# Other booked times for GpSimd, later sums of the key features, and another order of the last head's first products

## The chip, the cores and the metric

The kernel runs on one core of a Trainium2 chip. The metric is device time in microseconds (us) of one execution. A core has five engines that work at the same time and wait for each other through semaphores: TensorE (PE, matrix products), VectorE (DVE), ScalarE (ACT), GpSimd (POOL) and SyncE (SP, which issues DMAs; GpSimd issues some too). Each engine takes its own instructions in the order in which they were written.

## What is computed

The input is x (1 x 2048 x 1024), two sets of weights, and a gate vector. Block A is attention with a linear feature map, block B is softmax attention with 32 heads of 32 columns each, and a gate mixes both row by row:

```python
def _A_ref(x, wqkv, wo):          # H = 32, Dh = 32
    q, k, v = qkv[0], qkv[1], qkv[2]
    phi = lambda t: jnp.where(t > 0, t + 1, jnp.exp(t)) + 1e-6
    pq, pk = phi(q), phi(k)
    kv = jnp.einsum("bhsd,bhse->bhde", pk, v)
    z = jnp.einsum("bhsd->bhd", pk)
    num = jnp.einsum("bhqd,bhde->bhqe", pq, kv)
    den = jnp.einsum("bhqd,bhd->bhq", pq, z)[..., None] + 1e-6
    o = num / den
...
def _B_ref(x, wqkv, wo):
    scores = jnp.einsum("bhqd,bhkd->bhqk", q, k) * (Dh ** -0.5)
    p = _softmax(scores, axis=-1)
    o = jnp.einsum("bhqk,bhkd->bhqd", p, v)
...
g = _sigmoid((x * gate_w).sum(-1, keepdims=True))
return g * _A_ref(x, A_wqkv, A_wo) + (1 - g) * _B_ref(x, B_wqkv, B_wo)
```

## The kernel before

Up to about 620 us the kernel makes block B's q, k and v. From there on four kinds of work are woven into one another on TensorE, and the last stretch makes the output:

- `maxima`: score products (line 1440) whose maxima VectorE takes (1445), so that the exponentials stay small.
- `heads_`: for each of the 32 heads the score products (1581), the exponentials on ScalarE (1584) into nine buffers, the `pr` slots (big_5128 to big_5136), and the products of those with v (1731, in `av`), 16 blocks t of 128 keys in two calls, `av(0, 8)` and `av(8, 16)`, but in the last head in calls of four blocks.
- `linear`: block A's products. A weight is split into a rounded part and a rest, so every product takes three matmuls (lines 154, 157 and 159), and they come in chunks: key and value chunks kv0 to kv3, then the queries, then the output.
- the stores and the output stage.

The softmax's denominators are made with GpSimd's help. For each head it adds the exponentials of all blocks into one buffer `lacc` (big_5137 and big_5138 by turns): `first` (line 1662) adds blocks 0 and 1, `more` (1666) the rest, 128 x 1536 at a time, and the last four blocks in parts of 128 x 512; VectorE adds the remaining 512 columns. In heads 0 to 13 and 19 to 29 two DMAs that GpSimd issues (1620 and 1621, the "fold") then add one half of the partitions to the other, and TensorE sums over the partitions with small products against ones (1504, in `finish`). In the other heads `finish` reads the unfolded sums (1496). A head's `finish` is put into a list `ends` and is run at the start of the next head's `av(0, ...)`, so TensorE comes to it after it has done a good part of the next head's scores.

GpSimd also does three other things here: the rests of the weights at a change of chunk (`split_w`, 1054, behind a cast by ScalarE in 1052, eight of each at a change, each gated by TensorE's last use of the weight that is replaced; four changes: kv1 to kv2, kv2 to kv3, kv3 to the queries, and between the queries' two chunks), the sums of the key features (1331, or a copy in 1329 for a chunk's first block), and small sums for the gate (759).

Nothing of this order is fixed by hand. A planner in Python walks through the work and keeps a clock for each engine: `use(engine, cost, *after)` books a duration on the engine's clock T and gives back the time at which the result is there. GpSimd's additions are kept in a list `sums_left`, and `add_now` writes the next one when GpSimd's clock is no further than TensorE's; so the booked durations of GpSimd decide where its additions stand between the other work, and where the scores, products and finishes come on TensorE. `fold_now` writes a fold when its additions are booked as done, and books 6 us more until it has landed. The order is the only thing that the clocks leave in the program: what an engine really waits for is decided on the chip.

## Time and profile before

| | us |
|---|---|
| median of 3 runs | 2820.77 |
| lowest and highest | 2820.20 and 2821.47 |
| the profiled execution, its time | 2822.18 |
| the profiled execution, its span | 2820.4 |
| busy: TensorE | 2796.0 |
| busy: VectorE | 2268.8 |
| busy: GpSimd | 2102.9 |
| busy: ScalarE | 1662.6 |

The span is the time from the first to the last instruction in the trace. The profiled execution is 1.8 us longer than its span, and 1.4 us above the median. In the profile a row of the timeline has the start in us, the time that the row takes, the engine, the line, the operation and its tiles, how many instructions it holds (x3), and in brackets how long the engine was idle before it and what ended that. The table by windows gives for each stretch the busy time of each engine and the granted TensorE clock (PEclk, 1.00 is full speed). The waits are listed by who waited for whom, with the sum, the number and the longest of them.

### The profile page before, as it was taken

The numbers are of one execution on the slowest core, as the hardware profiler recorded it, in microseconds if no ns is written. First come the engines' busy times: TensorE is split into PE (matmuls) and PEld (weight loads), VectorE is DVE, ScalarE is ACT, GpSimd is POOL, SyncE is SP. The second block draws the span as 40 slices with busy tenths as digits, with TensorE's granted clock in tenths as the row PEclk, the third lists the DMA queues.
The fourth block names the chain that finished last, engine by engine and source line by source line (L and its number), as shares of the span: only waits on it lengthen the run. The fifth ranks groups of instructions, "written<-read, shape, count | busy, mean of one in ns | idle before, by whom it ended". The sixth has DMA issues, their size and how long they took to land.

```text
span 2820.4 us, 46781 instructions
## 1 busy us (share of the span) xinstructions
PE 2796.0 (99%) x15784; PEld 2010.3 (71%) x15784; DVE 2268.8 (80%) x3713; ACT 1662.6 (59%) x3170; POOL 2102.9 (75%) x1145
## 2 busy tenths in 40 slices
PE   9999999999999999999999999999999999999999
PEld 8888888886666666676676777667666666666587
DVE  6697759688877888788888778777888888887678
ACT  4343433347666666676776667667767667676522
POOL 0152026459999999999999789989999999999100
PEclk9999999999999999999999999999999999999999
DMA  8588749673433334333344456656544454334674
GB/s 269 166 275 281 225 143 283 218 234 90 123 84 84 92 99 111 93 98 89 88 117 129 152 158 193 183 170 195 136 108 131 107 162 107 92 106 126 233 232 155
DMA packets 391291, 432.77 MB, mean 153 GB/s; under 512 B 105550, under 2 KB 237902, under 8 KB 389260
## 3 DMA queue, kind: packets, MB, share of 16 engines
q1 hardware_dynamic: 367116, 389.27, 45.9%
q0 software_dynamic: 21632, 36.32, 6.1%
q10 hardware_dynamic: 2304, 4.20, 0.4%
q8 instruction: 126, 2.06, 0.3%
q14 instruction: 113, 0.93, 0.1%
HBM read 287.31 MB, written 127.93 MB: 147 GB/s over the span
## 4 chain that ended last, share of the span: by engine, by line
PE 90%; DVE 4%; POOL 3%; DMA 2%; ACT 1%; issue 1%; SPq 0%; DVEq 0%; POOLq 0%; ACTq 0%
PE bank L1731 15%; PE bank L1581 15%; PE bank L1440 15%; PE bank L154 12%; PE bank L157 12%; PE bank L159 12%; PE bank L644 5%; POOL big L1666 3%; DVE mx L1445 2%; DMA big<-ra 1%; PE bank L1504 1%; PE bank L1234 1%; DVE big L1903 1%; DMA big<-big 1%; ACT big L1584 1%
## 5 line engine op out<-in xcount | busy, mean ns | idle before, releaser
L1666 POOL TENSOR_TENSOR big<-big,big 128x512 f32<-128x512 f32 (+2 forms) x694 | 1643.7, 2372 | 61.0 <-ACT big L1584 15.0
L1445 DVE TENSOR_REDUCE mx<-bank 128x1 f32<-128x512 f32 x2048 | 1283.1, 682 | 280.6 <-PE bank L1440 278.3
L1584 ACT ACTIVATE big<-bank 128x512 f32<-128x512 f32 x2048 | 1151.7, 604 | 334.2 <-PE bank L1581 276.1
L1440 PE MATMUL bank<-big,big 128*128 128x512 f32 x1888 | 738.0, 393 | 2.9 <-ACT big L1584 2.2
L1581 PE MATMUL bank<-big,big 128*128 128x512 f32 x1888 | 736.4, 395 | 3.6 <-ACT big L1584 2.9
L154 PE MATMUL bank<-big,big 128*128 128x512 f32 x1408 | 552.8, 393 | 2.6 <-ACT big L304 1.4
L157 PE MATMUL bank<-big,big 128*128 128x512 f32 x1408 | 549.7, 390 | 0.0
L159 PE MATMUL bank<-big,big 128*128 128x512 f32 x1404 | 548.2, 390 | 1.1 <-DVE big L299 1.1
L1731 PE MATMUL bank<-big,mid 128*32 128x512 f32 x4096 | 457.6, 596 | 0.0
L1581 PEld LDWEIGHTS bank<-big,big 128*128 128x128 f32 x1888 | 353.3, 188 | 128.6 <-issue 43.6
L1440 PEld LDWEIGHTS bank<-big,big 128*128 128x128 f32 x1888 | 354.4, 188 | 84.1 <-ACT big L1584 7.7
L1731 PEld LDWEIGHTS bank<-big,mid 128*32 128x32 f32 x4096 | 133.8, 110 | 281.9 <-issue 279.9
L154 PEld LDWEIGHTS bank<-big,big 128*128 128x128 f32 x1408 | 264.8, 188 | 66.8 <-ACT big L1584 5.2
L159 PEld LDWEIGHTS bank<-big,big 128*128 128x128 f32 x1404 | 263.7, 188 | 57.3 <-DVE big L299 2.4
L157 PEld LDWEIGHTS bank<-big,big 128*128 128x128 f32 x1408 | 264.9, 188 | 55.2 <-DVE big L299 0.2
L1682 DVE TENSOR_TENSOR bank<-bank,big 128x512 f32<-128x512 f32 x364 | 252.2, 693 | 13.6 <-ACT big L1584 6.4
L304 ACT CAST big<-mid 128x512 fp32r<-128x512 f32 (+1 forms) x169 | 100.5, 619 | 138.1 <-DVE mid L1850 72.4
L299 DVE TENSOR_TENSOR big<-mid,big 128x512 fp32r<-128x512 f32 (+1 forms) x138 | 96.1, 712 | 78.6 <-ACT big L304 78.1
L644 PE MATMUL bank<-big,big 128*128 128x512 f32 x672 | 152.6, 389 | 0.0
L1662 POOL TENSOR_TENSOR big<-big,big 128x1536 f32<-128x1536 f32 (+1 forms) x31 | 132.9, 4288 | 24.0 <-ACT big L1584 24.0
L644 PEld LDWEIGHTS bank<-big,big 128*128 128x128 f32 x672 | 126.1, 188 | 26.2
L1739 ACT COPY mid<-bank 128x512 f32<-128x512 f32 x32 | 18.8, 588 | 207.9 <-PE bank L1731 180.5
(197 smaller groups left out, 2424.5 us busy)
## 6 DMA issues: line engine op xcount, KB each, us to landing
big<-xs SPq DMA_DIRECT2D x202, 256.0 KB
big<-qk SPq DMA_DIRECT2D x705, 64.0 KB
qk<-mid SPq DMA_DIRECT2D x128, 256.0 KB
xh<-xs SPq DMA_DIRECT2D x102, 256.0 KB
big<-oA SPq DMA_DIRECT2D x86, 256.0 KB
xs<-big SPq DMA_DIRECT2D x64, 256.0 KB
oA<-mid SPq DMA_DIRECT2D x64, 256.0 KB
big<-big POOLq DMA_DIRECT2D x50, 256.0 KB, 5.0
```

Source lines behind the costliest of these rows:

```text
L154: yield nc.tensor.matmul(ps, sh, mh_, start=(kt == 0), stop=False)
L157: yield nc.tensor.matmul(ps, sh, ml_, start=False, stop=(late and last))
L159: yield nc.tensor.matmul(ps, sl, mh_, start=False, stop=last)
L644: nc.tensor.matmul(bank[at + i], x_, w_, start=(kt == u == 0 and not onto), stop=(kt == KH - 1 and u == 2), skip_group_check=onto)
L1440: nc.tensor.matmul(bank[b], q[:, t % TPC * P:(t % TPC + 1) * P], k[:, j * C:(j + 1) * C], start=True, stop=True)
L1445: nc.vector.tensor_reduce(m[:, t, j:j + 1], bank[b], AX.X, ALU.max)
L1581: nc.tensor.matmul(bank[b], k[:, t * P:(t + 1) * P], q_cols(h, j), start=True, stop=True)
L1584: nc.scalar.activation(pr_t[i][:, j * C:(j + 1) * C], bank[b], AF.Exp, scale=SCALE)
L1662: nc.gpsimd.tensor_add(lacc[:, :qp], pr(0)[:, :qp], pr(1)[:, :qp])
L1666: nc.gpsimd.tensor_add(lacc[:, sl], lacc[:, sl], pr(t)[:, sl])
L1682: nc.vector.tensor_add(lacc[:, qp:] if t == NT - 1 else l_b[:, :n], l_b[:, :n], src)
L1731: nc.tensor.matmul(av_b[j * DH:(j + 1) * DH, :], v[:, t, :], pr(t)[:, j * C:(j + 1) * C], start=(t == 0), stop=(t == NT - 1))
```

## The change

Three edits.

The first is to durations that the planner books for GpSimd: a weight's rest 1.23 to 1.35; a key feature's sum 0.69 to 0.78; the two fold DMAs 2.0 to 2.45; `first` 0.15 to 0.96 plus 0.0022 for each column (for 1536 columns 3.53 to 4.34); `more` 0.15 to 0.21 plus the same.

The second takes the key features' sums out of the place where VectorE's feature is written, puts them into a list `z_todo`, and writes them in the main loop once TensorE's clock has passed the feature's booked end by 1.5.

The third concerns the last head only. Its first products with v, `av(0, 4)`, no longer wait for the finish of head 30 and no longer run it; that finish is run at the start of `av(4, 8)`.

```diff
-        w_ready[k] = use("dve", 0.6, end) if eng is nc.vector else use("pool", 1.23, end)
+        w_ready[k] = use("dve", 0.6, end) if eng is nc.vector else use("pool", 1.35, end)
...
     z_end = [0.0, 0.0]
+    z_todo = deque()
+
+    def features_now(upto=None):
+        while z_todo and (z_todo[0][0] <= upto if upto is not None else z_todo[0][1] <= T["pe"]):
+            z_todo.popleft()[2]()
...
             e, r = mid[3 + n % 3], mid[6]
+            features_now(n - 3)
...
-                def more(end, c=c, t=t, e=e, ps=ps):
+                def more(end, n=n, c=c, t=t, e=e, ps=ps):
                     pk = e[:, :HC]
                     nc.vector.scalar_tensor_tensor(pk, pk, 1.0, ps[:, :HC], op0=ALU.min, op1=ALU.add)
-                    z_end[c % 2] = use("pool", 0.69, end)
-                    if t == 0:
-                        nc.gpsimd.tensor_copy(zsum[c % 2], pk)
-                    else:
-                        nc.gpsimd.tensor_add(zsum[c % 2], zsum[c % 2], pk)
+                    z_end[c % 2] = None
+
+                    def features():
+                        z_end[c % 2] = use("pool", 0.78, end)
+                        if t == 0:
+                            nc.gpsimd.tensor_copy(zsum[c % 2], pk)
+                        else:
+                            nc.gpsimd.tensor_add(zsum[c % 2], zsum[c % 2], pk)
+
+                    z_todo.append((n, end + 1.5, features))
...
-            mark.end = use("pool", 2.0) + 6.0
+            mark.end = use("pool", 2.45) + 6.0
...
-            return use("pool", 0.15 + qp * 0.0022, at)
+            return use("pool", 0.96 + qp * 0.0022, at)
...
-            return use("pool", 0.15 + (sl.stop - sl.start) * 0.0022, at)
+            return use("pool", 0.21 + (sl.stop - sl.start) * 0.0022, at)
...
         def av(t0, t1):
             blocks_ = range(t0, t1)
+            early = last and t0 == 0
             yield lambda: both(max(pr_end[idx(blocks_[-1])], free[4] if t0 == 0 else 0.0),
-                               *(start() for start, _ in ends))
+                               *(start() for start, _ in ends if not early))
             use("pe", AV_SWITCH, pr_end[idx(blocks_[-1])])
-            while ends:
+            while ends and not early:
                 ends.pop()[1]()
...
         gate_step()
+        features_now()
         fold_now()
```

No engine has an instruction more or less; only the order differs. Lines after the edits are moved: in the changed kernel the finish's products are in lines 1508 and 1516 (before 1496 and 1504), the products with v in 1744 (1731), the fold in 1632 and 1633 (1620 and 1621), `first` in 1674 (1662), `more` in 1678 (1666), the score products in 1452 and 1593 (1440 and 1581), the features' sums in 1341 (1331).

Three places show how the order moves.

GpSimd, second chunk change, of before; head 7's additions go into big_5138, head 8's into big_5137; big_221, big_222, big_1258 and big_3332 hold the weights' parts, two columns each:

```order
L1666 TENSOR_TENSOR big_5138<-big_5138,big_5128 128x512
L1666 TENSOR_TENSOR big_5138<-big_5138,big_5129 128x512
L1620 DMA big_5138<-big_5138 64x4x256
L1621 DMA big_5138<-big_5138 64x4x256
L1662 TENSOR_TENSOR big_5137<-big_5130,big_5131 128x1536
L1054 TENSOR_TENSOR big_221<-big_5140,big_221 128x512
L1331 TENSOR_TENSOR mid_230<-mid_230,mid_227 128x256
L1054 TENSOR_TENSOR big_221<-big_5140,big_221 128x512
L1054 TENSOR_TENSOR big_222<-big_5140,big_222 128x512
```

The same place of the changed kernel, from the seventh of the eight rests (two for each of the four tiles) to the fold:

```order
L1054 TENSOR_TENSOR big_3332<-big_5140,big_3332 128x512
L1678 TENSOR_TENSOR big_5138<-big_5138,big_5135 128x512
L1678 TENSOR_TENSOR big_5138<-big_5138,big_5136 128x512
L1678 TENSOR_TENSOR big_5138<-big_5138,big_5128 128x512
L1678 TENSOR_TENSOR big_5138<-big_5138,big_5129 128x512
L1678 TENSOR_TENSOR big_5138<-big_5138,big_5135 128x512
L1054 TENSOR_TENSOR big_3332<-big_5140,big_3332 128x512
L1678 TENSOR_TENSOR big_5138<-big_5138,big_5136 128x512
L1678 TENSOR_TENSOR big_5138<-big_5138,big_5128 128x512
L1341 TENSOR_TENSOR mid_230<-mid_230,mid_228 128x256
L1678 TENSOR_TENSOR big_5138<-big_5138,big_5129 128x512
L1632 DMA big_5138<-big_5138 64x4x256
```

Before, all of head 7's additions, its fold and head 8's `first` come ahead of the first of the eight rests; in the changed kernel seven rests come ahead of the last eight additions, the eighth stands among them, and the fold stands behind them all.

GpSimd, first chunk change, of before, from head 1's last part of `more` (into big_5138):

```order
L1666 TENSOR_TENSOR big_5138<-big_5138,big_5132 128x512
L1054 TENSOR_TENSOR big_221<-mid_225,big_221 128x512
L1331 TENSOR_TENSOR mid_230<-mid_230,mid_229 128x256
L1620 DMA big_5138<-big_5138 64x4x256
L1621 DMA big_5138<-big_5138 64x4x256
L1054 TENSOR_TENSOR big_221<-big_5140,big_221 128x512
L1054 TENSOR_TENSOR big_222<-big_5140,big_222 128x512 x2
```

The same place of the changed kernel:

```order
L1054 TENSOR_TENSOR big_222<-big_5140,big_222 128x512 x2
L1054 TENSOR_TENSOR big_1258<-big_5140,big_1258 128x512
L1054 TENSOR_TENSOR big_1258<-mid_224,big_1258 128x512
L1054 TENSOR_TENSOR big_3332<-mid_225,big_3332 128x512
L1054 TENSOR_TENSOR big_3332<-big_5140,big_3332 128x512
L1678 TENSOR_TENSOR big_5138<-big_5138,big_5132 128x512
L1632 DMA big_5138<-big_5138 64x4x256
L1633 DMA big_5138<-big_5138 64x4x256
```

The fold moved from behind the first of the rests to behind the last.

TensorE, last head, of before; the finish of head 30 reads big_5137, the last head's products with v go into bank_242:

```order
L159 MATMUL bank_240<-big_1258,big_210 128x512
L1581 MATMUL bank_241<-big_208,big_209 128x512
L154 MATMUL bank_240<-big_1258,big_210 128x512
L157 MATMUL bank_240<-big_1258,big_210 128x512
L1496 MATMUL bank_243<-big_5137,ones 32x512 x4
L1731 MATMUL bank_242<-big_5129,mid_236 32x512 x4
L1731 MATMUL bank_242<-big_5130,mid_236 32x512 x4
L1731 MATMUL bank_242<-big_5131,mid_236 32x512 x4
L1731 MATMUL bank_242<-big_5132,mid_236 32x512 x4
L1581 MATMUL bank_245<-big_208,big_209 128x512
```

The same place of the changed kernel:

```order
L154 MATMUL bank_243<-big_3332,big_210 128x512
L1744 MATMUL bank_242<-big_5129,mid_236 32x512 x4
L1744 MATMUL bank_242<-big_5130,mid_236 32x512 x4
L1744 MATMUL bank_242<-big_5131,mid_236 32x512 x4
L1744 MATMUL bank_242<-big_5132,mid_236 32x512 x4
L1593 MATMUL bank_241<-big_208,big_209 128x512
```

The finish is gone from ahead of the products. It now stands behind 30 more matmuls, ahead of the next four blocks:

```order
L1593 MATMUL bank_243<-big_208,big_209 128x512
L157 MATMUL bank_244<-big_222,big_210 128x512
L159 MATMUL bank_244<-big_222,big_210 128x512
L1508 MATMUL bank_239<-big_5137,ones 32x512 x4
L1744 MATMUL bank_242<-big_5133,mid_236 32x512 x4
```

Two more facts of the changed order are used below. On TensorE, at the first chunk change, the last product with the weight that the eighth rest replaces stands 12 matmuls ahead of head 1's finish. At the second change, the last product with the weight that the seventh rest replaces stands 44 matmuls ahead of head 7's finish, and the last one with the eighth's five matmuls later. On ScalarE, there, the first exponential of head 8 into big_5135 stands between the casts of the seventh and the eighth weight; the score product that needs the bank which it empties comes eight matmuls behind the seventh's last product.

## The prediction

> **What bounds the kernel now.** I read the page's busy times first, then TensorE's waits, then the table by windows at the places of the waits, and there the timelines.
>
> ```profile
> PE 2796.0 (99%) x15784; PEld 2010.3 (71%) x15784; DVE 2268.8 (80%) x3713; ACT 1662.6 (59%) x3170; POOL 2102.9 (75%) x1145
> ```
>
> TensorE works 2796.0 of the span's 2820.4 us, and the change takes no matmul away. So all that an order can win is 24.4 us of idle time and what the clock loses behind it; it can lose any amount. Who TensorE waited for (us, times, longest):
>
> ```profile
> PE bank L1496 <- POOL big L1666: 5.4, 1, 5.4
> PE bank L1581 <- ACT big L1584: 2.9, 1, 2.9
> PE bank L1440 <- ACT big L1584: 2.2, 2, 1.4
> PE bank L1504 <- DMA big<-big: 1.8, 2, 1.1
> ```
>
> The windows show where, and that the clock falls behind each:
>
> ```profile
> core 0: us, PE busy (x) PEld busy (x) DVE busy (x) ACT busy (x) POOL busy (x), PEclk, DMA share, GB/s
> 764.00:784.00 20.00, 18.10 (x132) 9.02 (x131) 11.41 (x20) 9.42 (x20) 19.84 (x13) 0.91 0.45 103
> 796.00:804.00 8.00, 7.06 (x26) 4.14 (x25) 6.96 (x13) 3.84 (x8) 7.76 (x4) 1.00 0.14 40
> 1136.00:1156.00 20.00, 15.71 (x128) 9.32 (x130) 11.90 (x22) 10.27 (x22) 19.92 (x14) 0.91 0.44 116
> 2608.00:2624.00 16.00, 10.56 (x62) 5.02 (x61) 16.00 (x17) 6.96 (x15) 7.42 (x2) 0.89 0.91 318
> 2674.00:2690.00 16.00, 13.69 (x59) 10.37 (x58) 8.00 (x13) 4.34 (x8) 0.00 (x0) 1.00 1.07 356
> 650.00:1510.00 860.00, 850.76 (x5322) 572.95 (x5315) 708.40 (x1230) 581.89 (x1139) 833.69 (x413) 1.00 0.37 98
> ```
>
> Three places hold most of the loss: the first chunk change (idle 20 - 18.10 = 1.9 us), the second (4.3) and the last head (5.4). From 650 to 1510 us GpSimd works 833.69 of 860 us, so there it is nearly as full as TensorE, and where its work stands in its queue decides who waits.
>
> What a fallen clock costs is seen in the same 64 products with v, behind the first wait and undisturbed:
>
> ```profile
> 774.85 8.75 PE L1731 MATMUL bank<-big,mid 128*32 128x512 f32 x64
> ...
> 2595.47 0.39 PE L1581 MATMUL bank<-big,big 128*128 128x512 f32 x1
> 2595.70 0.39 PE L159 MATMUL bank<-big,xh 128*128 128x512 f32 x1
> 2596.02 7.07 PE L1731 MATMUL bank<-big,mid 128*32 128x512 f32 x64
> ```
>
> 8.75 - 7.07 = 1.7 us for one fall. I take 1.7 for each wait of about 2 us or more (1.9 was enough at 774 us); the 1.2 and 1.1 us from 2674 to 2690 us cost no clock (1.00):
>
> ```profile
> 2677.71 0.50 PE L154 MATMUL bank<-big,big 128*128 128x512 f32 x1 [1.19 <-ACT big L304]
> 2688.01 0.50 PE L159 MATMUL bank<-big,big 128*128 128x512 f32 x1 [1.12 <-DVE big L299]
> ```
>
> **The booked times.** What GpSimd's work takes, by the starts of neighbours:
>
> ```profile
> 953.15 1.01 POOL L1620 DMA_DIRECT2D big<-big x1 [0.30 <-POOL big L1666]
> 954.43 4.28 POOL L1662 TENSOR_TENSOR big<-big,big 128x1536 f32<-128x1536 f32 x1
> 957.89 1.51 POOL L1331 TENSOR_TENSOR mid<-mid,mid 128x256 f32<-128x256 f32 x1
> 944.83 8.02 POOL L1666 TENSOR_TENSOR big<-big,big 128x512 f32<-128x512 f32 x6
> 763.42 1.30 POOL L1054 TENSOR_TENSOR big<-mid,big 128x512 fp32r<-128x512 f32 x1
> 764.68 0.74 POOL L1331 TENSOR_TENSOR mid<-mid,mid 128x256 f32<-128x256 f32 x1
> ```
>
> A part of 512 takes 8.02 / 6 = 1.34 us; the new booking, 0.21 + 512 x 0.0022 = 1.34, meets it (the old said 1.28). A rest takes 764.68 - 763.42 = 1.26, booked 1.35. But the fold and `first` take 957.89 - 953.15 + 0.30 = 5.0 us together, and are booked at 2.45 + 4.34 = 6.8 (before 2.0 + 3.53 = 5.5). The 4.28 shown for `first` holds time that the fold's DMAs took from it; the next instruction starts 3.46 us after it. Over a head (12 parts and 10 long additions, each now booked 0.06 dearer) the old bookings ran short by about 22 x 0.06 - 0.5 = 0.8 us, and the new ones are 1.8 us too long. So the planner thought GpSimd ahead of where it was, and now thinks it behind: after five heads by about 9 us. It no longer writes GpSimd's additions where GpSimd could take them, but later, and puts other work in front.
>
> The Trainium skill, page "Perfetto Trace Analysis", section "GPSIMD Engine Instruction", says that a GpSimd span in a profile isn't to be trusted and that the spacing of starts is. By the span of 4.28 the booked 4.34 would be right; the 3.46 between two starts of this trace speaks for the page.
>
> **First chunk change, about 770 us.** In before the fold starts at 765.36 and TensorE waits 1.9 us in all:
>
> ```profile
> 765.36 0.97 POOL L1620 DMA_DIRECT2D big<-big x1
> 766.01 1.35 POOL L1621 DMA_DIRECT2D big<-big x1
> 772.40 0.59 PE L1504 MATMUL bank<-big,ones 64*32 64x256 f32 x2 [0.78 <-POOL big L1054]
> 774.11 0.66 PE L1504 MATMUL bank<-big,ones 64*32 64x256 f32 x14 [1.12 <-DMA big<-big]
> L1621 POOL DMA_DIRECT2D big<-big x25: 1008/1402/1431, 705.5 to 2559.9; - x25
> DMA to landing us min/median/max: 3.7/6.0/8.0
> ```
>
> Its price is 1.9 + 1.7 = 3.6 us. In the changed order the fold stands behind all eight rests and one part. The eighth rest needs TensorE's last product with the old weight, which is only 12 matmuls ahead of the finish; at 0.23 us a matmul (2595.70 - 2595.47 above) that is 2.7 us. From that product on: 0.2 us for the semaphore (an estimate), ScalarE's cast 0.62 (row below), the rest 1.3, the part 1.34, the wait 0.3, the second DMA's issue 766.01 - 765.36 = 0.65, its landing 6.0 by the median: 10.4 us. Less 2.7, TensorE waits 7.7 us (5.4 with the shortest landing, 9.7 with the longest), and 1.7 for the clock: 9.4. Against before **+5.8**.
>
> **Second chunk change, about 1140 us.** In before ScalarE's cast waited, put down to a load (whose buffer the rests free), and TensorE with it, as the exponentials stand behind the cast:
>
> ```profile
> 1136.69 2.05 POOL L1054 TENSOR_TENSOR big<-big,big 128x512 fp32r<-128x512 f32 x1
> 1141.44 0.62 ACT L1052 CAST big<-big 128x512 fp32r<-128x512 f32 x1 [3.54 <-DMA big<-in_a_wqkv]
> 1142.60 0.49 PE L1581 MATMUL bank<-big,big 128*128 128x512 f32 x1 [2.88 <-ACT big L1584]
> 1148.90 0.50 PE L1440 MATMUL bank<-big,big 128*128 128x512 f32 x1 [1.41 <-ACT big L1584]
> ```
>
> GpSimd came to the rests only at 1136.69. Price: 2.88 + 1.41 + 1.7 = 6.0. The new order removes this wait, since the rests come first. It puts two in its place. Count from the end of the last product with the seventh weight. GpSimd: semaphore, cast and rest, 0.2 + 0.62 + 1.3 = 2.1; then five parts, 6.7: 8.8. Only then is big_5135 free for head 8's exponential (0.6 with semaphores): 9.5 us. TensorE needs that exponential's bank eight matmuls (1.8 us) after the same product, so it waits 7.7. The eighth cast stands behind that exponential on ScalarE: cast 0.62, rest 1.3, two parts 2.7, a feature's sum 0.7, a part 1.34, wait 0.3, DMA 0.65 and landing 6.0 bring the fold to 23.1. TensorE reaches the finish after 44 matmuls (10.0) plus the 7.7: it waits another 5.4 (3.1 to 7.4 by the landing). With two falls of the clock 7.7 + 5.4 + 3.4 = 16.5, against before **+10.5**. What this leaves for head 8: its copy of a chunk's first features (1339) stands after only five additions and can wait for its chunk's unit.
>
> ```profile
> POOL mid L1331 <- DVE mid L1326: 7.0, 3, 5.4
> ```
>
> Such waits took 7.0 / 3 = 2.3 us (0 to 5.4); the second fall of the clock gives GpSimd 1.7 of it: **+0.6** (0 to +3.7). The third change (kv3 to the queries) has its rests spread among the additions and the fold well behind; I put nothing on it (0 to +3, a wait as in the first place of before).
>
> **Last head.**
>
> ```profile
> 2593.59 21.91 POOL L1666 TENSOR_TENSOR big<-big,big 128x1536 f32<-128x1536 f32 x6
> 2603.72 7.95 ACT L1584 ACTIVATE big<-bank 128x512 f32<-128x512 f32 x16
> 2609.73 0.39 PE L157 MATMUL bank<-big,big 128*128 128x512 f32 x1
> 2615.56 1.94 PE L1496 MATMUL bank<-big,ones 128*32 128x512 f32 x8 [5.44 <-POOL big L1666]
> 2617.26 4.15 PE L1731 MATMUL bank<-big,mid 128*32 128x512 f32 x32
> ```
>
> TensorE is out of work at 2609.73 + 0.39 = 2610.12, and GpSimd's additions for head 30 end at 2615.50. The products with v need only the exponentials, whose 16 end at 2603.72 + 7.95 = 2611.67; the first three blocks' are done by 2609.8 (12 of 16). So `av(0, 4)` starts between 2610.1 and 2611.7: idle 0 to 1.6, I take 0.8. Its 32 products take half of 7.07, 3.5 us, and the 30 matmuls behind it 6.8: the finish comes at about 2621, 5.7 us after GpSimd is done, so nothing waits there. Gain 5.44 - 0.8 = 4.6 and the clock's 1.7: **-6.3** (-5.5 to -7.1). An idle 1.6 lies between the 1.2 that cost no clock from 2674 to 2690 and the 1.9 that did; if the clock falls, the gain is 3.8. The Trainium skill, page "TensorE: Matmul & The Clock Gate", section "HAM oscillation — how this bites in real kernels", puts the limit at idle gaps of about 3.4 us; by it 1.6 costs nothing and the gain is at least 5.5. But 1.9 us at 774 was enough here, and no run here has 1.6, so I keep both ends.
>
> **What is left.** TensorE's matmuls change between the large products and other kinds five times more often (143 stretches against 138); the products with v start 0.32 after the last matmul (2596.02 - 2595.70) where 0.23 is the spacing; five times 0.09, +0.5 (0 to +1). Of the 0.9 us lost from 796 to 804 I count half as gone: -0.5 (0 to -0.9). The features' sums themselves are the same instructions.
>
> **The sum.** +5.8 + 10.5 + 0.6 - 6.3 + 0.5 - 0.5 = +10.6. The profiled execution 2822.2 gives 2832.8; the median lies 1.4 lower: **2831.4**. With the shortest landings (-4.6), one fall of the clock less (-1.7) and the lower ends of the rest (-2.3) it is 2822.8; with the longest (+4.0) and the upper ends (+3.1 for head 8, +3 for the third change, +2.5 for the last head), 2844.
>
> **Rivals.** A, faster: GpSimd's real time per head follows the bookings (contention makes `first` cost 4.3 wherever it stands). Then the planner no longer thinks GpSimd ahead, and the waits for it go: 3.6 + 6.0 at the two changes, 6.3 in the last head, 0.5 more: 2820.8 - 16.4 = 2804.4. The point is whether GpSimd still has work in its queue when the rests come; the 3.46 spacing speaks against, the 2.88 and 1.41 us that TensorE waited behind a GpSimd late with the rests for. Chance 0.13.
>
> B, about the same: the waits at the changes are as long as before, because GpSimd, ahead of the planner, has the rests done sooner and the landing is short; only the last head counts: 2814.5. Against it stands that the eighth rest can't start before TensorE's own product. Chance 0.17.
>
> C, slower still: each later fold of a chunk's head (eight more) also waits about 2 us behind a feature's sum, with a fall of the clock at half of them: 2831.4 + 16 + 7 = about 2854. For it, features' sums now stand right ahead of a fold in some heads; against it, the longest wait of that kind was 5.4 in 860 us. Chance 0.07.
>
> **Chances.** The forecast, 0.63, has its own range of 2822 to 2842. Two tenths of a per cent, about what a measurement of this kernel can tell from no change, is 5.6 us: 2815.1 and 2826.4. Faster: A's 0.13 and half of B, 0.22. Within: B's other half and the forecast's low end, 0.17. Slower: the rest, 0.61. The range runs from 2812, below B, to 2842; outside lie A and most of C.
>
> **What would show it.** Right: in the changed trace 1516's first product waits over 5 us near 770 us for a fold behind line 1054; near 1140 us there are two waits over 4 us, the first in 1593 for an exponential that waited for line 1678, the second in 1516; in the last head 1508 waits for nothing and 1744 starts within 1.6 us. Wrong: waits of 2 us or less at 1516 near 770, or GpSimd without a gap ahead of the rests near 1130.

## The result and the profile after

The changed kernel takes 2852.34 us (median of 4 runs, 2850.56 to 2854.89) against 2820.78: a ratio of 1.0112, 95% interval 1.0095 to 1.0130. It is slower by 31.6 us. The forecast had the way right (+10.6, slower) and a third of the size; 2852 lies outside its range of 2812 to 2842.

The page of the changed kernel, busy times:

```profile
span 2853.0 us, 46780 instructions
PE 2814.6 (99%) x15784; PEld 2008.3 (70%) x15784; DVE 2267.9 (79%) x3713; ACT 1648.7 (58%) x3170; POOL 2104.4 (74%) x1145
```

TensorE has the same 15784 matmuls and is busy 18.6 us longer (2814.6 against 2796.0); its idle time grew by 14.0 only (38.4 against 24.4). More than half of the loss hides in the busy time: work at a lower clock, and short waits. A matmul is shown with 0.39 us where the next one starts 0.23 after it, so a wait of up to 0.16 ahead of a matmul still counts as busy.

Its longest waits by TensorE (us, times, longest), to be read against the four shown of before:

```profile
PE bank L1516 <- DMA big<-big: 8.8, 7, 3.2
PE bank L1593 <- ACT big L1596: 8.2, 2, 7.4
PE bank L154 <- DMA big<-xs: 2.3, 1, 2.3
```

The wait for GpSimd in the last head is gone; the waits for folds went from 1.8 to 8.8, those of score products for ScalarE grew to 7.4 in one piece. The windows at the two changes of chunk and over GpSimd's full stretch (columns as in the table of before):

```profile
764.00:784.00 20.00, 15.69 (x112) 7.82 (x114) 14.43 (x26) 9.83 (x22) 18.44 (x13) 0.83 0.40 89
1140.00:1170.00 30.00, 19.66 (x125) 11.57 (x127) 16.85 (x30) 10.97 (x23) 26.64 (x17) 0.83 0.30 66
650.00:1510.00 860.00, 835.42 (x5128) 551.58 (x5121) 687.45 (x1190) 556.35 (x1102) 797.39 (x388) 0.99 0.35 93
```

First change: idle 4.3 and a clock of 0.83, where before had 1.9 and 0.91. Second: idle 10.3 of 30 us. GpSimd, busy 833.69 of the 860 us in before, is busy 797.39 and so idles 36 us more.

Where the time went is read best from the start of each head's finish on TensorE (first product of line 1504 or 1516, or 1496 or 1508; starts in us from the timeline; the difference is called the lag below):

| | head 6 | 7 | 8 | 9 | 10 | 17 | 20 | 29 | end of span |
|---|---|---|---|---|---|---|---|---|---|
| before | 1083.18 | 1150.75 | 1210.23 | 1270.54 | 1330.52 | 1849.21 | 2044.90 | 2568.87 | 2820.4 |
| changed | 1089.52 | 1161.80 | 1231.56 | 1297.85 | 1359.48 | 1878.36 | 2081.32 | 2606.56 | 2853.0 |
| later by | 6.3 | 11.1 | 21.3 | 27.3 | 29.0 | 29.2 | 36.4 | 37.7 | 32.6 |

So 6.3 us are lost up to head 6 (the first change lies in it), 22.7 from head 6 to head 10, 8.7 from there to head 29, and 5.1 come back at the end. The profiled runs are 2.6 us (changed) and 1.4 us (before) above their medians, so a single lag is good to a microsecond or two.

The two places that the prediction described look as it said. GpSimd and TensorE at the first change, changed kernel:

```profile
770.20 1.28 POOL L1054 TENSOR_TENSOR big<-big,big 128x512 fp32r<-128x512 f32 x1 [0.20 <-ACT big L1052]
771.44 1.28 POOL L1678 TENSOR_TENSOR big<-big,big 128x512 f32<-128x512 f32 x1
773.01 1.01 POOL L1632 DMA_DIRECT2D big<-big x1 [0.30 <-POOL big L1678]
```

```profile
776.82 1.03 PE L1516 MATMUL bank<-big,ones 64*32 64x256 f32 x2 [3.18 <-DMA big<-big]
778.71 1.10 PE L1516 MATMUL bank<-big,ones 64*32 64x256 f32 x14 [0.86 <-DMA big<-big]
```

The eighth rest, a part, the fold, and TensorE waiting for it. At the second change, GpSimd, ScalarE and TensorE:

```profile
1130.02 1.29 POOL L1054 TENSOR_TENSOR big<-big,big 128x512 fp32r<-128x512 f32 x1 [3.08 <-ACT big L1052]
1132.01 1.29 POOL L1054 TENSOR_TENSOR big<-big,big 128x512 fp32r<-128x512 f32 x1 [0.69 <-ACT big L1052]
...
1143.18 6.50 POOL L1678 TENSOR_TENSOR big<-big,big 128x512 f32<-128x512 f32 x5
...
1157.78 1.01 POOL L1632 DMA_DIRECT2D big<-big x1 [0.30 <-POOL big L1678]
```

```profile
1149.71 0.60 ACT L1596 ACTIVATE big<-bank 128x512 f32<-128x512 f32 x1 [7.84 <-POOL big L1678]
```

```profile
1150.36 0.80 PE L1593 MATMUL bank<-big,big 128*128 128x512 f32 x1 [7.37 <-ACT big L1596]
1161.80 0.59 PE L1516 MATMUL bank<-big,ones 64*32 64x256 f32 x2 [0.79 <-DMA big<-big]
1164.56 0.90 PE L1516 MATMUL bank<-big,ones 64*32 64x256 f32 x14 [2.18 <-DMA big<-big]
1165.84 8.25 PE L1744 MATMUL bank<-big,mid 128*32 128x512 f32 x64
```

GpSimd idles ahead of each rest while five parts stand behind them that it could take (they read slots of which it has already added another part); the exponential waits for these parts, TensorE for the exponential (7.37, forecast 7.7), and then for the fold (0.79 + 2.18 = 3.0, forecast 5.4).

### The profile page after: what moved, and what is told of

The parts are those of the page before. It is cut to its first block, busy times and chain, and to the rows that moved or that the text cites. A ratio compares the mean times of both kernels' runs of the same rounds, so it can differ in the third digit from the quotient of the medians.

```text
span 2853.0 us, 46780 instructions
## 1 busy us (share of the span) xinstructions
PE 2814.6 (99%) x15784; PEld 2008.3 (70%) x15784; DVE 2267.9 (79%) x3713; ACT 1648.7 (58%) x3170; POOL 2104.4 (74%) x1145
## 4 chain that ended last, share of the span: by engine, by line
PE 90%; DVE 4%; DMA 2%; POOL 2%; ACT 1%; issue 1%; SPq 0%; POOLq 0%; DVEq 0%; ACTq 0%
PE bank L1744 16%; PE bank L1593 15%; PE bank L1452 14%; PE bank L154 13%; PE bank L157 13%; PE bank L159 12%; PE bank L644 5%; DVE mx L1457 3%; POOL big L1678 1%; ACT big L1596 1%; DMA big<-big 1%; PE bank L1516 1%; PE bank L1240 1%; DVE bank L1694 1%; DMA big<-ra 0%
## 5 line engine op out<-in xcount | busy, mean ns | idle before, releaser
L1596 ACT ACTIVATE big<-bank 128x512 f32<-128x512 f32 x2048 | 1139.7, 606 | 359.5 <-PE bank L1593 293.0
L1593 PE MATMUL bank<-big,big 128*128 128x512 f32 x1888 | 728.8, 396 | 10.6 <-ACT big L1596 8.2
```

The costliest lines, as they stand in the source:

```text
L1593: nc.tensor.matmul(bank[b], k[:, t * P:(t + 1) * P], q_cols(h, j), start=True, stop=True)
L1596: nc.scalar.activation(pr_t[i][:, j * C:(j + 1) * C], bank[b], AF.Exp, scale=SCALE)
```

## The experiments

Lags in this section are starts of finishes against before, as in the table, in the profiled run of each kernel. Ratios are to before in the same session.

**Which edit costs.** Three kernels with a part of the change each, and one with all of it at other durations.

e1, the last head's edit alone:

```diff
+            early = last and t0 == 0
...
-                               *(start() for start, _ in ends))
+                               *(start() for start, _ in ends if not early))
...
-            while ends:
+            while ends and not early:
```

> The kernel before with the last head's edit alone: av(0, 4) of the last head ahead of head 30's finish; bookings and features' sums as before. GpSimd's order is that of before. Theory (the loss is GpSimd's, made between 770 and 1350 us; the last head gains by itself): 2820.8 - 6.3 = 2814.5, between 2813 and 2816, and TensorE's 5.44 us wait at 2615 gone. Rival (the last head's gain only pays back what the rest of the change delayed): 2819 to 2822.

Measured 2821.57 against 2821.34, ratio 0.9997 (0.9989 to 1.0006): nothing. The wait at 2615 is gone, but another stands 10 us behind it. TensorE and VectorE there:

```profile
2619.72 1.07 PE L1496 MATMUL bank<-big,ones 128*32 128x512 f32 x8
2630.02 1.04 PE L1581 MATMUL bank<-big,big 128*128 128x512 f32 x2 [4.45 <-DVE mid L1517]
```

```profile
2604.55 24.82 DVE L1686 TENSOR_TENSOR big<-big,big 128x512 f32<-128x512 f32 x28 [9.15 <-ACT big L1584]
2629.29 0.67 DVE L1517 TENSOR_TENSOR mid<-mid,bank 128x512 f32<-128x512 f32 x1
```

The finish keeps a bank until VectorE has multiplied by its result (line 1517), and that stands behind 28 of VectorE's own sums for the last head. A score product needs the bank.

e2, the booked durations alone (only the calls are shown, not their whole lines):

```diff
-use("pool", 1.23, end)
+use("pool", 1.35, end)
-use("pool", 0.69, end)
+use("pool", 0.78, end)
-mark.end = use("pool", 2.0) + 6.0
+mark.end = use("pool", 2.45) + 6.0
-use("pool", 0.15 + qp * 0.0022, at)
+use("pool", 0.96 + qp * 0.0022, at)
-use("pool", 0.15 + (sl.stop - sl.start) * 0.0022, at)
+use("pool", 0.21 + (sl.stop - sl.start) * 0.0022, at)
```

> The kernel before with the five booked durations alone. Theory (the bookings of the fold and of the first addition, 1.8 us a head too long, let the planner write rests and features' sums in front of additions that GpSimd could take; GpSimd, full in this stretch, then idles and never wins it back): nearly the whole loss is here, 2820.8 + 31.6 + 6.3 = 2858.7, between 2845 and 2862, with the fold of head 1 behind the rests and GpSimd idle 15 us or more from 1120 to 1240. Rival 1 (the later features' sums cost it, by the 8.2 us that their copy waits in head 8 and by sums ahead of folds): 2818 to 2828. Rival 2 (VectorE's maxima came late by another order on TensorE and VectorE, and GpSimd only followed): 2825 to 2840.

Measured 2881.28, ratio 1.0210 (1.0196 to 1.0224): 59.9 us, nearly twice the changed kernel's loss of 31.6, and above the expected range, which ended at 2862. Its GpSimd, full stretch, and at the copy of the last chunk's first features:

```profile
650.00:1510.00 860.00, 819.80 (x4932) 532.90 (x4925) 660.88 (x1142) 530.62 (x1055) 770.49 (x378) 0.97 0.34 89
```

```profile
1204.28 0.40 POOL L1329 COPY mid<-mid 128x256 f32<-128x256 f32 x1 [11.90 <-ACT big L1584]
```

e3, the later features' sums alone (`features_now` and its two calls as in the change, the old 0.69):

```diff
-                    z_end[c % 2] = use("pool", 0.69, end)
...
+                    def features():
+                        z_end[c % 2] = use("pool", 0.69, end)
...
+                    z_todo.append((n, end + 1.5, features))
```

> The kernel before with the later features' sums alone; bookings and last head as before. Both folds at the chunk changes stand ahead of the rests, as in before. Theory (bookings): 2816 to 2826, no wait at a chunk change above 4 us. Rival 1 (the later sums): 2840 to 2855, with a wait of GpSimd for a feature's sum or copy of 5 us or more.

Measured 2816.92, ratio 0.9983 (0.9974 to 0.9992): 4.4 us less than before. This edit is a gain, not the loss; with the new bookings it takes back nearly half of what they cost (2881 to 2855 in e7 below, which has both and not the last head's edit).

e4, the changed kernel with two durations as the starts in the trace have them:

```diff
-            mark.end = use("pool", 2.45) + 6.0
+            mark.end = use("pool", 1.58) + 6.0
-            return use("pool", 0.96 + qp * 0.0022, at)
+            return use("pool", 0.08 + qp * 0.0022, at)
```

> The changed kernel with two numbers put to the starts in the trace: fold 1.58 instead of 2.45, first addition 0.08 plus 0.0022 a column instead of 0.96 plus the same, 5.0 us together instead of 6.8. All else as changed. Theory: the folds stand ahead of the rests again at both chunk changes, GpSimd keeps its work, and the last head's gain stays: 2808 to 2818, and GpSimd's idle time from 1120 to 1240 under 6 us. Rival 1 (the later features' sums): 2838 to 2855. Rival 2 (another order on TensorE and VectorE): 2825 to 2845.

Measured 2813.93, ratio 0.9973 (0.9962 to 0.9983). The fold at the second change stands ahead of the rests again (it starts at 1126.64, the changed kernel's at 1157.78), and GpSimd is full:

```profile
650.00:1510.00 860.00, 853.07 (x5349) 577.94 (x5342) 713.84 (x1238) 587.14 (x1148) 834.05 (x413) 1.00 0.38 99
```

So the loss comes from the 1.75 us a head by which the fold and the first addition are booked too long (0.87 and 0.88; which of the two matters more was not tried). What stays open after these four is how. Bookings that are too short cost little: e3 has the old ones, 0.8 us a head short by the prediction's count, and stands at 0.9983, while e8 below, which is e3 with durations nearer to the trace, stands at 0.9973.

**Is GpSimd full?** e6, before with five long additions of head 4 done twice:

```diff
             nc.gpsimd.tensor_add(lacc[:, sl], lacc[:, sl], pr(t)[:, sl])
+            if h == 4 and 4 <= t <= 8:
+                nc.gpsimd.tensor_add(lacc[:, sl], lacc[:, sl], pr(t)[:, sl])
```

> The kernel before with five long additions of head 4 (blocks 4 to 8) done twice, so head 4's denominators count them twice; not booked, so the order is otherwise that of before. It takes 17.9 us of GpSimd's time. Theory (GpSimd has next to no slack from 650 to 1510): the time grows by nearly that, plus a fall of the clock or two: 12 to 21 us, 2833 to 2842, without one instruction more on TensorE. Rival (GpSimd has slack, as TensorE is busy 99%): under 4 us, 2821 to 2825.

Measured 2839.34 against 2821.51, ratio 1.0061 (1.0047 to 1.0074): 17.8 us more for 17.9 us of GpSimd's time. GpSimd has no slack there, though TensorE counts as busy 99%. An exponential in this kernel that waits for a doubled addition (line 1668), and two waits of TensorE:

```profile
928.71 1.08 ACT L1584 ACTIVATE big<-bank 128x512 f32<-128x512 f32 x2 [4.68 <-POOL big L1668]
929.36 0.79 PE L1581 MATMUL bank<-big,big 128*128 128x512 f32 x1 [4.55 <-ACT big L1584]
966.88 0.79 PE L1440 MATMUL bank<-big,big 128*128 128x512 f32 x1 [4.64 <-ACT big L1584]
```

TensorE does not wait for GpSimd by name: the exponentials wait for slots that GpSimd has not read, and TensorE for the exponentials.

**What is lost in heads 8 to 10.** If that were all, GpSimd time given back in head 8 would return. e5 leaves out five of its additions, e10 its two feature sums, e11 both:

```diff
-            nc.gpsimd.tensor_add(lacc[:, sl], lacc[:, sl], pr(t)[:, sl])
+            if not (h == 8 and 6 <= t <= 10):
+                nc.gpsimd.tensor_add(lacc[:, sl], lacc[:, sl], pr(t)[:, sl])
```

```diff
                         z_end[c % 2] = use("pool", 0.78, end)
+                        if c == 3 and t < 2:
+                            return
```

> The changed kernel with five of GpSimd's long additions of head 8 (blocks 6 to 10) left out, so head 8's denominators lack them; the planner books them all the same, so the order is otherwise that of the changed kernel. It gives GpSimd 5 x 3.58 = 17.9 us in the place where the changed kernel loses most. Theory (GpSimd is full, so each us that it idles at the second change is paid by TensorE in heads 8 and 9, and GpSimd time given back there comes back as time): 13 to 18 us less, 2834 to 2839. Rival (TensorE loses in heads 8 and 9 because VectorE's maxima and ScalarE's exponentials were put into another order by the wait; GpSimd only follows): 2846 to 2853.

> The changed kernel with the two feature sums that stand among head 8's additions left out (the copy of the last chunk's first features and the sum of its second ones), so block A's denominators lack them. Booked all the same; the rest of the order is that of the changed kernel. After the run with a short head 8 showed no gain, two readings are left. Theory (the place of these two in GpSimd's queue: the copy makes GpSimd idle 8.2 us, and the sum, whose feature comes late, has nine parts and the fold behind it): head 8's fold starts 8 us or more earlier, 2842 to 2848. Rival (TensorE, VectorE and ScalarE wait for each other in heads 8 and 9 by their own order, GpSimd has time): 2850 to 2854.

> Both left out: the two feature sums and five long additions of head 8. Nothing of GpSimd's can then be late in head 8. Theory (GpSimd's queue, by place and by volume together): the loss of heads 8 to 10 (17.9 us in the profile) is gone but for what the clock's fall behind head 7's finish costs, 2833 to 2841. Rival (their own order on the other engines): 2848 to 2854.

Measured 2852.86 (ratio 1.0111, 1.0095 to 1.0126), 2850.87 (1.0108, 1.0092 to 1.0123) and 2851.30 (1.0106, 1.0092 to 1.0120), each about the changed kernel's 2852.34. My theory falls for this place: in e5 GpSimd spends the time that it was given idle, and in e11 even head 8's fold, 23 us earlier, brings next to nothing. GpSimd in e5, then in e11:

```profile
1212.36 0.74 POOL L1341 TENSOR_TENSOR mid<-mid,mid 128x256 f32<-128x256 f32 x1 [18.92 <-ACT big L1596]
```

```profile
1202.09 1.01 POOL L1634 DMA_DIRECT2D big<-big x1 [0.30 <-POOL big L1681]
1227.82 0.74 POOL L1343 TENSOR_TENSOR mid<-mid,mid 128x256 f32<-128x256 f32 x1 [23.69 <-DVE mid L1333]
```

Two readings were left: that it follows from head 7's wait, or that it is in the order of the score products on TensorE. There are two kinds of these: those for the maxima (line 1452 of the changed kernel) and those for the exponentials (1593), called scores here. The table goes through them in the written order, from one head's finish to the next, and counts how often one follows another of its own kind, whatever stands between them:

| up to the finish of head | 7 | 8 | 9 | 10 |
|---|---|---|---|---|
| before | 0 | 0 | 0 | 2 |
| changed | 21 | 50 | 38 | 21 |
| e2 (bookings alone) | 27 | 46 | 38 | 21 |
| e3 (features' sums alone) | 0 | 0 | 0 | 2 |
| e4 (real spacings) | 0 | 4 | 4 | 2 |

Before alternates: a maximum, a score, and so on, with other products between. The changed kernel has runs of three to seven of a kind. As I read the planner, it held scores back for slots that it thought GpSimd still needed; no run shows that step by itself. What a run costs is seen on TensorE at 1251 us, changed kernel:

```profile
1251.15 0.39 PE L154 MATMUL bank<-big,xh 128*128 128x512 f32 x1
1251.38 2.16 PE L1452 MATMUL bank<-big,extra 128*128 128x512 f32 x5
1253.89 0.50 PE L1593 MATMUL bank<-big,big 128*128 128x512 f32 x1 [0.35 <-DVE mx L1457]
```

Five products whose own time is 5 x 0.23 = 1.15 take to 1253.89, 2.5 us, and only 0.35 of it is shown as idle. TensorE's weight loads name what they waited for from 1170 to 1335 us (us, times, longest):

```profile
PEld bank L1452 <- DVE mx L1457: 6.9, 18, 1.0
PEld bank L1593 <- DVE mx L1457: 3.3, 8, 0.7
PEld bank L1452 <- ACT big L1596: 2.9, 7, 0.7
PEld bank L1593 <- ACT big L1596: 1.7, 3, 1.3
```

Together these four are 14.8 us. In before, from 1160 to 1360 us, weight loads waited 0.2 us for the maxima (line 1445), and those of score products 0.9 for exponentials.

e14 takes head 7's wait for the exponential away and keeps the order; e15 makes what a run waits for shorter and keeps the order:

```diff
-        eng.tensor_sub(lo, raw, f32(hi))
+        if not (kind == "kv" and c == 3 and eng is nc.gpsimd):
+            eng.tensor_sub(lo, raw, f32(hi))
```

```diff
-nc.vector.tensor_reduce(m[:, t, j:j + 1], bank[b], AX.X, ALU.max)
+nc.vector.tensor_reduce(m[:, t, j:j + 1], bank[b][:, :C // 2] if 8 <= h <= 11 else bank[b], AX.X, ALU.max)
```

> The changed kernel with GpSimd's eight weight rests of the second change (kv2 to kv3) left out, so block A's last key and value chunk uses old rests; ScalarE's casts stay, all orders are otherwise those of the changed kernel. Head 7's two waits must go with their falls of the clock (14.7 us lost from 1140 to 1170): that both readings expect. Open is what heads 8 to 10 lose after it (about 17 us from 1180 to 1330), which neither five additions less nor two feature sums less brought back. Theory (the order of the score products on TensorE: in heads 7 to 10 they stand in runs of equal kind, three to seven maxima or scores in a row, as the planner held them back for a GpSimd that it thought late; each run waits a little for VectorE's maxima or ScalarE's exponentials, whatever GpSimd does): that loss stays, 2852.3 - 14 = 2838, between 2833 and 2842. Rival (it all follows from head 7's wait, which throws the engines out of step): 2820 to 2828.

> The changed kernel with VectorE's maxima of heads 8 to 11 taken over 256 of the 512 columns of each score block, so these maxima miss half the scores (they only keep the exponentials small); no booking and no order changes. TensorE's weight loads waited there, from 1170 to 1335 us, 6.9 + 3.3 us for line 1457. Theory (runs of equal score products wait for VectorE and ScalarE): this part of the loss goes, 6 to 10 us less, 2842 to 2847, and what waits for ScalarE and for folds stays. Rival (VectorE isn't what TensorE waits for; its waits only mark that everything is out of step): 2850 to 2854.

e14 measured 2846.60 (ratio 1.0091, 1.0074 to 1.0108), 5.7 less and not the 14 that I had put on it: the wait for the exponential is gone, but a feature's sum now stands ahead of head 7's last part and fold with nothing in front of it, and the fold is late by that. GpSimd in e14:

```profile
1148.43 0.74 POOL L1342 TENSOR_TENSOR mid<-mid,mid 128x256 f32<-128x256 f32 x1 [12.08 <-DVE mid L1334]
1149.13 1.29 POOL L1679 TENSOR_TENSOR big<-big,big 128x512 f32<-128x512 f32 x1
1150.72 1.01 POOL L1633 DMA_DIRECT2D big<-big x1 [0.30 <-POOL big L1679]
```

Still it tells the two readings apart. Behind head 7's finish and all its waits, at the end of the products with v, its lag is 8.8 (changed kernel 15.4). From there to head 10 it loses 22.5 - 8.8 = 13.7 us, where the changed kernel loses 29.0 - 15.4 = 13.6, and the four waits of its weight loads, from 1164 to 1330 us, are the same to a tenth (6.9, 3.3, 2.9 and 1.7). The later loss doesn't depend on how large the earlier one was.

e15 measured 2846.78 (ratio 1.0089, 1.0072 to 1.0106), 5.6 us less. At the end of head 7's products with v its lag is 12.9, so 2.5 of its gain lie ahead of that, and from there to head 10 it loses 22.1 - 12.9 = 9.2 instead of 13.6. Its weight loads there:

```profile
PEld bank L1452 <- DVE mx L1457: 1.4, 4, 0.4
PEld bank L1593 <- DVE mx L1457: 0.8, 2, 0.4
PEld bank L1593 <- ACT big L1596: 4.0, 8, 1.3
PEld bank L1452 <- ACT big L1596: 3.5, 7, 0.9
```

The waits for VectorE fell from 10.2 to 2.2, those for ScalarE grew from 4.6 to 7.5. So about a third of the loss in heads 8 to 10 (4.4 of 13.6) is shown to be waits for VectorE's maxima, which before with its alternating order doesn't have. That the rest is runs that wait for ScalarE, and folds, is argued from the rows and from e4, whose order is regular and which loses nothing there (lag -5.1 at head 6, -6.1 at head 10). No kernel was run with the changed kernel's bookings and a regular order of the score products.

**The last head.** e7 is the changed kernel without the last head's edit, e8 is e4 without it; both diffs are that of e1 turned round.

> The changed kernel without the last head's edit: the finish of head 30 runs ahead of av(0, 4) again. Theory (GpSimd's additions for head 30 set the end of the stretch; TensorE's delays between head 18 and 20 had already eaten the wait, and the edit is worth next to nothing): 2852.3 + 0.6, between 2851 and 2855. Rival (the prediction's step, the edit is worth 6.3 in the changed kernel): 2857 to 2861.

> The kernel with real spacings (fold 1.58, first addition 0.08 plus 0.0022 a column, features' sums later) without the last head's edit. Theory: the edit is worth 1 to 2 here (its kernel ended 7.9 earlier than before in the profile, where GpSimd's folds were 6.4 earlier), 2814 to 2817. Rival (6.3): 2819 to 2822.

Measured 2854.55 (2853.55 to 2855.32; the changed kernel 2850.56 to 2854.89) and 2814.16 (e4: 2813.93). By the medians the edit is worth 2.2 in the changed kernel, by the ratios to before (1.0116 and 1.0112) 1.1, which the spread of the runs does not settle; it is worth nothing in e4. The changed kernel's GpSimd and TensorE there:

```profile
2597.79 50.33 POOL L1678 TENSOR_TENSOR big<-big,big 128x1536 f32<-128x1536 f32 x14
```

```profile
2647.96 3.64 PE L1744 MATMUL bank<-big,mid 128*32 128x512 f32 x32
2658.64 1.07 PE L1508 MATMUL bank<-big,ones 128*32 128x512 f32 x8
```

GpSimd is done at 2597.79 + 50.33 = 2648.12 and TensorE comes to the place at 2647.96: with the old order it would have waited 0.2 us, and in e7, which has the old order, no wait shows there. TensorE's delays had used up the wait.

e12 is e1 with VectorE's multiplication six sums earlier, e13 the same on e4:

```diff
-        f_left[:] = chain(fns, end, 3)
+        f_left[:] = chain(fns, end, 1 if h == H - 2 else 3)
...
-                    items = chain([(lambda _, j=j: add_last(t, j), 0.61) for j in range(NJ)], pr_end[idx(t)], 2)
+                    items = chain([(lambda _, j=j: add_last(t, j), 0.88 if t < 9 else 0.61) for j in range(NJ)], pr_end[idx(t)], 2)
```

> The kernel before with the last head's edit, and VectorE's multiplication behind head 30's finish (line 1517) moved ahead of six of its own sums (the sums of blocks below 9 are booked at 0.88, as they ran there, and the multiplication gets a higher rank). Theory (the edit alone gained nothing because this multiplication, which frees a bank for the scores, stood behind 28 sums of VectorE that ran at 0.89 us each): the 4.45 us wait and the clock's fall behind it go, 2821.6 - 6.1 = 2815.5, between 2814 and 2818. Rival (GpSimd's additions for head 30 set the end of the stretch anyway, another wait takes its place): 2820 to 2822.

> The kernel with real spacings (fold 1.58, first addition 0.08 plus the columns) with the same move of VectorE's multiplication. Its wait there was 1.48 us without a fall of the clock. Theory: 2813.9 - 1.4 = 2812.5, between 2811 and 2814.5. Rival: no change, 2813.5 to 2815.

Measured 2814.99 (ratio 0.9981, 0.9972 to 0.9990) and 2811.89 (0.9968, 0.9955 to 0.9980). In e12 the wait for line 1517 is 1.15 where e1 had 4.45, and nearly all of the 6.3 that the prediction put on the edit is there: 5.8 less than before in the same session, where e1 was 0.2 more. VectorE in e12:

```profile
2605.69 21.53 DVE L1686 TENSOR_TENSOR big<-big,big 128x512 f32<-128x512 f32 x22 [9.18 <-ACT big L1584]
2627.14 0.67 DVE L1517 TENSOR_TENSOR mid<-mid,bank 128x512 f32<-128x512 f32 x1
```

e13, at 2811.89, is the fastest of all, 9 us below before (2820.75).

## Why the prediction was right or wrong

| term | forecast | measured (lags of the table) |
|---|---|---|
| first change (measured: all up to head 6) | +5.8 | +6.3 |
| second change, head 7's two waits and the clock | +10.5 | +9.1 |
| heads 8 to 10 | +0.6 | +13.6 |
| heads 11 to 29 | 0 | +8.7 |
| last head and end | -6.3 | -5.1 |
| sum | +10.6 (with +0.5 and -0.5 for the rest) | +32.6 |

The second row's 9.1: the 64 products with v behind head 7's finish end at 1165.84 + 8.25 = 1174.1 in the changed kernel; in before they start at 1151.62 and take 7.09, to 1158.7. That is a lag of 15.4, less the 6.3 of head 6. The third row is 29.0 - 15.4.

**The booked times and the two changes of chunk** were right in mechanism, and near in size: rests ahead of the additions, an exponential behind the additions, a cast behind the exponential, and a fold behind all. The bookings, read against the starts in the trace, did tell which way the planner would err (e4, e2). Of the signs that the prediction named, the waits came in their places but shorter: 3.18 at the first change where it said over 5, and 7.37 and 3.0 at the second where it said two over 4. At the first change single pieces were off against each other, and that the sum fits is in part luck. TensorE waited 3.18 + 0.86 = 4.0 for the fold, not 7.7: the fold's second half landed 5.1 us after its issue and not 6.0, and TensorE took 4.5 us and not 2.7 for the twelve matmuls ahead of the finish, five of them a run of maxima that took 2.50. The clock, in turn, was at half for 6.8 us, of which 4.9 were work: 2.4, where I had 1.7. Behind the first change (the end of head 1's first products with v) the lag is 4.8, at head 2 it is 2.3, and up to head 6 it grows again to 6.3, in heads where the changed order has more runs than before (48 and 28 repeats up to the finishes of heads 2 and 3, before 28 and 18).

**The step that failed most** is "What this leaves for head 8", +0.6 with an upper end of +3.7, where +13.6 was measured. It looked for a wait that could be named, GpSimd's copy behind its unit, and that one did come (8.2 us of idle GpSimd), but it cost little: without it and the next sum, e10 is at most 1.5 us faster. What I did not price, and put at nothing without a reason, is that the same bookings also decide how TensorE's own products are ordered in the heads around the change. Runs of score products wait there for VectorE's maxima (4.4 of the 13.6, by e15) and, as argued above, for ScalarE. I had compared how much of each work TensorE had done at each head, and found it the same; the sequence within a head was not looked at. It is in the written order for anyone to count: 0, 0, 0, 2 against 21, 50, 38, 21.

**The last head** was wrong as a step, and that its number nearly came is luck. "The products with v need only the exponentials ... Gain 5.44 - 0.8 = 4.6 and the clock's 1.7" holds for the wait that is there in before; alone (e1) it gains nothing, because the finish's bank is freed by a multiplication that stands behind VectorE's sums, and the prediction did not follow the finish beyond TensorE. In the changed kernel the wait was gone before the edit could take it (e7).

**Heads 11 to 29**, put at nothing. The third change, for which an upper end of +3 was allowed, cost nothing (lag 29.4 at head 11, 29.2 at head 17). Of the 8.7, 3.5 come between heads 17 and 18, where TensorE waits 2.29 for a load at 1920 us and the clock falls; why the load is late was not tried and stays open. Another 3.7 come between heads 18 and 20, and there runs return: up to the finishes of heads 19 and 20 the changed kernel has 16 and 22 repeats, before 8 and 6. e4 has 12 and 18 there and loses 3.7 as well, e3 has 8 and 6 and loses 0.2; so the good bookings leave this piece, and it goes with the runs, though nothing else tests it. All of it was free in the end: TensorE's lag of 37.7 at head 29 falls to 32.6, as the wait for GpSimd in the last head is no longer there.

**The rivals.** A (GpSimd's real time follows the bookings) fell with e4: with the starts' 5.0 us the order is good. B (waits at the changes as before) fell with the rows of both changes: 4.0 and 10.3 us, before 1.9 and 4.3. Of C, slower still, the size came near (2854 against 2852), its mechanism did not: the features' sums are a gain (e3).

## What to carry to other kernels

A booked duration for an engine that is full decides more than where its own work stands: here the planner, thinking GpSimd late, also bunched the products of TensorE. So book such an engine by the spacing of starts; too short was the safer side here (1.75 us a head too long cost 38, 0.8 too short about 3). After a change of bookings look at the written sequence of the engine that is bound (does it still alternate?), not only at its amounts. A share of busy time of 99% on one engine says little about the slack of another: 17.9 us more on GpSimd, busy 97%, cost 17.8, and waits of up to 0.16 us a product never showed as idle. An edit that removes a wait must be followed to whatever gives back the resources it now takes later, here a bank behind another engine's queue.

## What the runs showed of the hardware

A sum by VectorE with both inputs in SBUF (the core's own memory) ended only as GpSimd's running addition ended. In e1 the first three of VectorE's 28 sums for the last head take 1.97 and twice 3.94 us, beside GpSimd's last additions for head 30; the 25 behind them, with GpSimd done, start 0.60 apart. VectorE, GpSimd, VectorE:

```profile
2604.55 1.97 DVE L1686 TENSOR_TENSOR big<-big,big 128x512 f32<-128x512 f32 x1 [9.15 <-ACT big L1584]
2606.44 7.87 DVE L1686 TENSOR_TENSOR big<-big,big 128x512 f32<-128x512 f32 x2
```

```profile
2606.05 7.72 POOL L1666 TENSOR_TENSOR big<-big,big 128x1536 f32<-128x1536 f32 x2
```

```profile
2614.24 15.13 DVE L1686 TENSOR_TENSOR big<-big,big 128x512 f32<-128x512 f32 x25
```

GpSimd's two end at 2613.77, VectorE's third at 2614.31. In before it is the same (2.52 and twice 3.89 us, then 0.6). So the 0.89 a sum that the expectation of e12 names is a mean of three very slow ones and many of 0.60. The Trainium skill, page "GPSIMD Engine Reference", section "Specifications", lists SBUF interfaces that GpSimd shares with VectorE and names instructions with two inputs in SBUF among those that contend; these sums have two, and the rows agree.

In every trace of this case, from 640 us on, each fall of the granted clock to 0.50 lasted 3.41 us or a whole multiple of it (6.83 or 10.24), but for those that the end of the span cut short. A wait's length alone did not tell whether it fell: 2.18 us at 1914 in e14 cost no clock, 2.07 at 2718 in the changed kernel did, and 0.78 + 1.12 at 772 in before did. So the prediction's 1.7 for each wait of about 2 us or more is right for one fall of 3.41 us, and not for every wait.
